# A fixed order for the whole program, output matmuls in column halves, and inputs laid out ahead

## The chip, the cores and the metric

One core of one Trainium2 chip runs the whole program. The metric is the device time of one execution in microseconds. TensorE is called PE here, VectorE DVE, ScalarE ACT, GpSimd POOL and SyncE SP.

## What is computed

Three stages in float32, one behind another: a linear attention with complex decay, a dense MLP, and a mixture of 8 experts with two experts to a token. Cut to what matters:

```python
# attention: B, H, S, D = 4, 8, 768, 48
mag = sqrt(a_re**2 + a_im**2); scale = minimum(mag, 0.999) / (mag + 1e-6)
for t in range(S):                                   # S: complex state [D, D] per head
    S_re, S_im = ar*S_re - ai*S_im + outer(k[t], v[t]), ar*S_im + ai*S_re
    y[t] = q[t] @ S_re
x = y.transpose(0, 2, 1, 3).reshape(3072, 384)
# dense MLP: d_ff = 2048; w_in and w_out arrive as float64
h = x @ w_in; g = where(h > 0, h, exp(minimum(h, 0)) - 1); x = g @ w_out
# experts: F = 1024
logits = x @ w_gate + log1p(exp(x @ w_noise)) * noise
top2 and their softmax weights; out[t] = sum of weight * (maximum(x[t] @ w1[e], 0) @ w2[e])
```

## The kernel before

**Attention** runs in units: a chunk of 128 steps for two of the four batches (`i` = 0, 1), 12 units in all, six chunks. Per unit the factors are made on ACT and DVE (`p_pieces`), the angles are summed on PE with a triangular matrix (L280), and the sizes are transposed on PE (L302) and multiplied up on DVE (L311 to L322). `kk` and `qq` (L371, L383) transpose the unit's k and q on PE, four transposes of a pair of heads each, since q and k are loaded with the steps on the partitions; DVE then reads the transposed q and k from PSUM (L372, L384). `sc` (L463) makes the scores, DVE masks them (L467). `y` (L480, L482) makes the output: for each of 8 heads one matmul with the carried state (`Sc`, from the second chunk on) and one with the masked scores `P`, each with 128 stationary columns and 48 moving. `upd` (L424) makes the state's update `pu`, with 64 stationary columns at a time. `xt` (L496 to L498) transposes the output and splits it in a high and a low part, `xh` and `xl`.

**The MLP** of a unit (`f_pieces`) multiplies in three passes of split float32: `ph` at L531 (256 moving columns), the activation on ACT and DVE (L535 to L541), then `y` at L555 (400 columns, of which 16 are the gate's). Its weights are loaded, decoded from float64 on DVE (L144 to L146, L161) and split with PE's help (L186 to L205) in the start. `route` picks the experts of a chunk and writes a table by indirect DMAs on POOL (L647).

**The experts** come last: for each of 8, rows are gathered by POOL (L728), transposed (L733), multiplied at L748 (`mph`), activated (L750, L751) and multiplied at L770 (`mpo`, one tile of 128 tokens each); the results are added to those of the experts before and scattered (L775, L778).

**The order** is set by priorities. `PAR` gives each class of pieces a window of time in the unit's clock, `place` and `settle` turn that into a priority, and the framework places whatever is ready by priority on the engines, matmul by matmul, with a timing of its own. Each engine then works its list from front to back. SP and POOL issue the loads from lists of that kind. `load` (L108 to L122) issues one DMA per tile: q and k go into tiles padded to 64 columns, which POOL first clears (L117); a_re and a_im come in one DMA each; all read runs of 48 values.

Of the kernel before, what the change touches and what calls it, by code (L numbers as in the profile page):

```python
# [21 lines left out]

@with_exitstack
def tile_kernel(ctx, tc, q, k, v, a_re, a_im, w_in, w_out, w_gate, w_noise, noise, w1, w2, out, dbg=None):
# [3 lines left out]
    L = 128  # L28
# [5 lines left out]
    F = w_in.shape[1]  # L34
# [25 lines left out]
    # ---------------------------------------------------------------- constants  # L60
# [32 lines left out]
    nc.vector.memset(nat["a"][:, :, :, :, D:], 0.0)  # L93
# [16 lines left out]
    def load(n, u, i):  # L110
        if n == "v":
            t = V[u, i] = wa.tile([128, Dm], F32, name="vt", tag="vt", bufs=2)
            to = t.rearrange("p (h d) -> p h d", h=H)
        else:
            if n in "qk":
                t = nat[n, u, i] = wa.tile([128, H, 64], F32, name=n, tag="n4", bufs=4)
                nc.gpsimd.memset(t[:, :, D:], 0.0)  # L117
            else:
                t = nat["a"][:, i, int(n == "ai")]
            to = t[:, :, :D]  # L120
        src = srcs[n]
        nc.sync.dma_start(to, bass.AP(tensor=src.tensor, offset=src.offset + bat(u, i) * H * S * D + chunk(u) * L * D,  # L122
                                      ap=[[D, L], [S * D, H], [1, D]]))
# [4 lines left out]
    # ---------------------------------------------------------------- weights of the first MLP  # L128
# [37 lines left out]
    def w_in_piece(f, a, b, raw):  # L166
        src = w_in.rearrange("(c p) f -> p c f", p=128)[:, a // 128:b // 128, f * 128:(f + 1) * 128]
        if wide:
            return raw.rearrange("p (c f) x -> p c (f x)", f=128), src.bitcast(I32)
        return raw.rearrange("p (c f) -> p c f", f=128), src  # L170
# [36 lines left out]
    # ---------------------------------------------------------------- attention, factors of a unit  # L207
    V, X, KK, ET = {}, {}, {}, {}

    def p_pieces(u):  # L210
        """per step: the logarithm of the squared factor and the tangent of half its angle"""
# [3 lines left out]
        def start():  # L215
            for i in range(NB):
                load("ar", u, i)
                load("ai", u, i)
# [29 lines left out]
    def t_pieces(ua, us):  # L248
        """cosines and sines of unit us, angles of unit ua: together, for the sake of the tables"""
# [20 lines left out]
    def o_pieces(u):  # L270
        """sums of the angles (twice the halves) in turns, less the whole turns, negated"""
# [18 lines left out]
    def m_pieces(u):  # L290
        """products of the factors' sizes"""
# [43 lines left out]
    def a_pieces(u):  # L335
# [20 lines left out]
        def by_head(x, t):  # L356
            """planes of real and imaginary parts, a pair's heads in the halves of the partitions,
            to planes of the heads, real and imaginary parts in the halves"""
            copy = nc.vector.tensor_copy
            copy(t[:64], x[64:, 0])  # L360
            copy(x[64:, 0], x[:64, 1])
            copy(x[:64, 1], t[:64])

        def kk(i):
            def f():
                x, k = X[u], KK[u, i]
                b = k[:, 1]
# [6 lines left out]
                by_head(k, nat["k", u, i].rearrange("p (q j) d -> p q (j d)", j=2))  # L374
            return f

        def qq(i):
            def f():
                x, b = X[u], ET[u]
                o = slice(i * HP, (i + 1) * HP)  # L380
                tp = psa.tile([128, HP, 128], F32, name="tp", **ring("qq"))
                for p in range(HP):
                    nc.tensor.transpose(tp[:, p, :], pairs(nat["q", u, i], p), ident)  # L383
                tt(b[:, o], b[:, o], tp, op=OP.mult)  # L384
# [11 lines left out]
    # ---------------------------------------------------------------- attention, products of a unit  # L396
    def b_pieces(u):
# [73 lines left out]
        def y(i):  # L471
            def f():
                b = bat(u, i)
                py = psa.tile([128, Dm], F32, name="py", **ring("y"))
                for p in range(HP):
                    for j in range(2):
                        h = 2 * p + j
                        oh = slice(h * D, (h + 1) * D)
                        if c:
                            mm(py[:, oh], X[u][:, j, i * HP + p, :], Sc[i][:, p, j, :], start=True, stop=False,  # L480
                               skip_group_check=True)
                        mm(py[:, oh], d["P", i, j][:, p, :], V[u, i][:, oh], start=not c, stop=True,  # L482
                           skip_group_check=True)
# [29 lines left out]
    # ---------------------------------------------------------------- first MLP of a unit  # L513
# [154 lines left out]
    # ---------------------------------------------------------------- mixture of experts  # L668
    FE = w1.shape[2] // 128
# [21 lines left out]
    def e_weight(e, f, n):  # L691
# [3 lines left out]
        if n == 0:  # L695
            nc.sync.dma_start(raw.rearrange("p (c f) -> p c f", c=KD),
                              w1[e].rearrange("(c p) f -> p c f", p=128)[:, :, f * 128:(f + 1) * 128])
# [86 lines left out]
    # ---------------------------------------------------------------- order of work  # L784
# [7 lines left out]
    def place(cls, u, pieces):  # L792
        """a class's pieces of a unit lie one after another in its window of time"""
# [9 lines left out]
    def settle(rules):  # L803
        """moves pieces to later times until all that use a thing come after what makes it"""
# [139 lines left out]
    def check():  # L944
        """flags: something for the general path, the first slot that is still open, slots per expert"""
# [48 lines left out]
    # ---------------------------------------------------------------- what the fast path left  # L994
# [3 lines left out]
    def rest(first):  # L998
        for e in range(E):
            with ExitStack() as st:  # L1000
# [19 lines left out]
                for f in range(FE):  # L1020
                    wa = gw.tile([128, KD, 128], F32, name="gwa")
                    nc.sync.dma_start(wa, w1[e].rearrange("(c p) f -> p c f", p=128)[:, :, f * 128:(f + 1) * 128])
# [13 lines left out]
    def redo():  # L1036
        """attention step by step, the first MLP and the routing for any values"""
# [140 lines left out]
    with tc.If(load_reg(0, 1) != 0):  # L1178
# [7 lines left out]
        "moe2_noise", "moe2_w1", "moe2_w2"]  # L1186
# [26 lines left out]
```

## Time and profile before

| | |
|---|---|
| median of 3 runs | 1281.93 us (1280.65 to 1283.49) |
| span of the profiled execution | 1274.1 us |
| PE busy | 1202.6 us, 94% |
| DVE busy | 797.9 us, 63% |
| ACT busy | 655.1 us, 51% |
| POOL busy | 251.8 us, 20% |
| HBM read, written | 80.69 MB, 20.70 MB |

The profile is of one execution; the span runs from its first to its last instruction. Matmuls are pipelined, so their durations overlap: what a matmul takes of PE is the distance from its start to the next start, not the mean duration in a group. A float32 matmul stands in the trace as two records, a transpose or a split one as one. The start up to the first `ph` takes some 125 us, attention and MLP together go on to about 775 us, the experts take the rest.

### The profile page before, as it was taken

Reading aid. Unit: us, or ns where it says so; the run is one execution under the profiler, and the core shown is the slowest. Engines: PE = TensorE matmul, PEld = TensorE weight load, DVE = VectorE, ACT = ScalarE, POOL = GpSimd, SP = SyncE. Lnnn points to the kernel's source line nnn. Section 1 sums busy time; section 2 is a strip of 40 time slices with the busy share of each in tenths; the row PEclk is TensorE's granted clock in tenths of the full one; section 3 lists DMA queues with packets and bytes.
Section 4 is the critical chain, followed back from the end, with each engine's and each line's share of the span. In section 5 each row is a group of like instructions: output and inputs, shape, how many; then the busy total and the mean of one; then the engine's idle time right before and its main releaser. Section 6 shows DMA issues by size and latency. Waiting matters only on the chain. (4 is left out here: it accounts for less than half of the span.)

```text
span 1274.1 us, 21830 instructions
## 1 busy us (share of the span) xinstructions
PE 1202.6 (94%) x8309; PEld 1132.9 (89%) x8309; DVE 797.9 (63%) x1783; ACT 655.1 (51%) x1299; POOL 251.8 (20%) x313
## 2 busy tenths in 40 slices
PE   3687999999999999999998999899999999999996
PEld 3475999999999999999998998899898989899995
DVE  6999958687887888788787557253434334353221
ACT  8768847476666857675663366142323333241110
POOL 3211000110020011002000400633333242424221
PEclk9788989899999999999999999899999999999998
DMA  9854121122131222213111134242425243332111
GB/s 269 231 134 113 32 55 27 40 37 57 23 57 36 45 46 43 57 20 57 26 32 33 32 119 125 80 130 87 139 90 145 86 129 106 109 113 83 42 44 33
DMA packets 192179, 100.71 MB, mean 79 GB/s; under 512 B 143231, under 2 KB 182886, under 8 KB 192064
## 3 DMA queue, kind: packets, MB, share of 16 engines
q1 hardware_dynamic: 177456, 59.36, 19.7%
q0 software_dynamic: 14608, 39.86, 10.3%
q8 instruction: 67, 1.10, 0.4%
q14 instruction: 48, 0.39, 0.1%
HBM read 80.69 MB, written 20.70 MB: 80 GB/s over the span
## 5 line engine op out<-in xcount | busy, mean ns | idle before, releaser
L751 DVE SCALAR_TENSOR_TENSOR egl<-mph,egh 128x320 fp32r<-128x320 f32 (+1 forms) x128 | 74.6, 587 | 158.7 <-ACT egh L750 158.7
L750 ACT ACTIVATE egh<-mph 128x320 fp32r<-128x320 f32 (+1 forms) x128 | 65.1, 514 | 210.4 <-PE mph L748 172.7
L770 PE MATMUL mpo<-weh,egh 128*128 128x384 f32 (+1 forms) x448 | 153.8, 343 | 0.4 <-ACT egh L750 0.4
L770 PE MATMUL mpo<-wel,egh 128*128 128x384 f32 (+1 forms) x448 | 151.4, 338 | 0.0
L555 PE MATMUL y<-woh,gh 128*128 128x400 f32 x384 | 138.2, 360 | 0.4 <-ACT gh L540 0.3
L555 PE MATMUL y<-wol,gh 128*128 128x400 f32 x384 | 133.9, 349 | 0.0
L555 PE MATMUL y<-woh,gl 128*128 128x400 f32 x384 | 125.1, 357 | 0.0
L770 PE MATMUL mpo<-weh,egl 128*128 128x384 f32 (+1 forms) x448 | 122.3, 338 | 0.0
L702 DVE TENSOR_TENSOR wel<-raw,weh 128x384 fp32r<-128x384 f32 x128 | 70.1, 556 | 71.0 <-ACT weh L701 65.9
L701 ACT ACTIVATE weh<-raw 128x384 fp32r<-128x384 f32 x128 | 66.2, 525 | 88.8 <-PE mph L748 62.8
L531 PE MATMUL ph<-xh,wih 128*128 128x256 f32 x576 | 105.5, 289 | 3.1 <-DVE route L635 1.5
L531 PE MATMUL ph<-xl,wih 128*128 128x256 f32 x576 | 106.9, 285 | 0.0
L531 PE MATMUL ph<-xh,wil 128*128 128x256 f32 x576 | 105.7, 285 | 0.0
L647 POOL DMA_INDIRECT table<-route x48 | 52.1, 1085 | 208.1 <-DVE route L638 195.3
L540 ACT ACTIVATE gh<-ge 128x512 fp32r<-128x512 f32 x96 | 60.5, 630 | 61.6 <-DVE ge L537 57.8
L778 POOL DMA_INDIRECT out_dram<-ac,slots x56 | 55.1, 984 | 184.0 <-DVE ac L775 158.4
L531 PEld LDWEIGHTS ph<-xh,wih 128*128 128x128 f32 x576 | 85.7, 190 | 4.8 <-DVE ge L537 2.3
L531 PEld LDWEIGHTS ph<-xl,wih 128*128 128x128 f32 x576 | 85.5, 190 | 0.0
L531 PEld LDWEIGHTS ph<-xh,wil 128*128 128x128 f32 x576 | 85.1, 190 | 0.0
L770 PEld LDWEIGHTS mpo<-weh,egh 128*128 128x128 f32 (+1 forms) x448 | 81.2, 181 | 3.6 <-ACT egh L750 0.7
L770 PEld LDWEIGHTS mpo<-wel,egh 128*128 128x128 f32 (+1 forms) x448 | 81.1, 181 | 2.9
L770 PEld LDWEIGHTS mpo<-weh,egl 128*128 128x128 f32 (+1 forms) x448 | 77.9, 180 | 4.7
(214 smaller groups left out, 2884.2 us busy)
## 6 DMA issues: line engine op xcount, KB each, us to landing
raw<-in_moe_w_dram SPq DMA_DIRECT2D x128, 192.0 KB, 2.6
raw<-in_moe_w_in_dram POOLq DMA_DIRECT2D x16, 384.0 KB, 4.2
raw<-in_moe_w_out_dram POOLq DMA_DIRECT2D x16, 384.0 KB, 4.0
nat_a<-in_a_re_dram SPq DMA_DIRECT2D x24, 192.0 KB, 3.9
nat_a<-in_a_im_dram SPq DMA_DIRECT2D x24, 192.0 KB, 2.8
vt<-in_v_dram SPq DMA_DIRECT2D x24, 192.0 KB, 2.7
q<-in_q_dram SPq DMA_DIRECT2D x24, 192.0 KB, 4.5
k<-in_k_dram SPq DMA_DIRECT2D x24, 192.0 KB, 2.8
```

The costliest lines, as they stand in the source:

```text
L531: mm(ph[:, j, :], w[:, z, :], x[:, z, :], start=n == 0, stop=n == 3 * KD - 1)
L540: act(gh, e, AF.Copy)
L555: mm(d["y"][i], g[:, j, i * L:(i + 1) * L], w, start=s == 0 and j == 0 and n == 0, stop=s == NS - 1 and j == 1 and n == 2)
L647: st = nc.gpsimd.indirect_dma_start(out=table[:, :], out_offset=bass.IndirectOffsetOnAxis(ap=idx, axis=0), in_=row, in_offset=None)
L701: act(w[0], raw, AF.Copy)
L702: tt(w[1], raw, w[0].bitcast(F32), op=OP.subtract)
L750: act(gs[0][:, f, :n], ph[:, :n], AF.Relu)
L751: stt(gs[1][:, f, :n], ph[:, :n], 0.0, gs[0][:, f, :n].bitcast(F32), op0=OP.max, op1=OP.subtract)
L770: mm(po[:m], x[:, f, o:o + m], w, start=k == 0, stop=k == 3 * FE - 1)
L778: sc = nc.gpsimd.indirect_dma_start(out=out[:, :], in_=ac[:m], in_offset=None, out_offset=bass.IndirectOffsetOnAxis(ap=st[:m, t, 0:1], axi ...
```

## The change

Three things change.

**A fixed order.** A new function `arrange` runs when the program up to the end of the experts has been recorded. It finds what each instruction must wait for (data, PSUM banks, buffers of a pool), gives each a duration from a table of its own, and plans one list for each engine: whenever an engine is free, it takes, of what is ready, the piece with the longest chain of work behind it, and from the check of the flags on simply the first one in the program. Consecutive matmuls into one tile are kept together as a run. It then ties each instruction to the one before it in its engine's list, so that the lists stand as planned. In its table (`cost`) the first number is the time until the next instruction may start, the second the duration, both in ns; `pr` is the priority. The 28 DMAs that clear outputs are held back to a later time of the plan.

**Column halves.** Each output matmul of `y` is issued as two, for the first and the second 64 of the 128 stationary columns, one after the other.

**Inputs laid out ahead.** `kernel()` passes q and k already transposed by pairs of heads and padded (`q_pairs`, `k_pairs`), v with the heads side by side, a_re and a_im padded and in one array, and `moe_w_in` and `moe2_w1` in blocks of 128 columns. The old q, k, v, a_re and a_im still go in for the general path, which does not run on these inputs. The 192 transposes, the memsets of q, k and the factors' padding go; the factors' two DMAs per tile become one.

```diff
+def arrange(tc):
+    ins = [i for i in nc.cur_bb.bb.instructions if type(i).__name__ != "BassTilePoolBoundary"]
...
+    def cost(n):
...
+            if i.tile_size[1] != 128 or i.tile_size[0] != 128:
+                return 72, 229
+            return (223, 387) if cols <= 128 else (1.72 * cols, 1.72 * cols + 170)
...
+        if e == "PE" and p is not None and kinds[n] == kinds[p] == "Matmult":
+            same = a[0] == b[0]
+            r32 = "32r" in str(i.ins[0].dtype)
+            if same and (not r32 or not i.start_tensor_calc):
+                run[n] = run[p]
...
+    for h in reversed(todo):
+        tail[h] = sum(step[z] for z in members[h][:-1]) + dur[members[h][-1]] + 34 + max((tail[x] for x in out[h]), default=0)
+    pr = {h: -tail[h] if h < cut else 1e9 + h for h in heads}
...
+        if kinds[h] == "DMACopy" and any(x[0].startswith("zero_") for x in acc[h]):
+            r = max(r, 90000.0 + 2000.0 * len(zeros))
...
+    while done < len(heads):
+        for e in E:
...
+        while cand[e] and cand[e][0][0] <= t:
+            r, p, h = heapq.heappop(cand[e])
+            heapq.heappush(now[e], (p, h))
+        p, h = heapq.heappop(now[e])
...
+        for z in order:
+            for y in before[e]:
+                tc.add_manual_dep(ins[z], ins[y].name, how, reason="order")
...
     def load(n, u, i):
+        if n == "a":
+            t = nat["a"][:, i]
+            nc.sync.dma_start(t.rearrange("p x h d -> p (x h d)"), ap[u, i])
+        elif n == "v":
             t = V[u, i] = wa.tile([128, Dm], F32, name="vt", tag="vt", bufs=2)
+            nc.sync.dma_start(t, vp[u, i])
         else:
-            if n in "qk":
-                t = nat[n, u, i] = wa.tile([128, H, 64], F32, name=n, tag="n4", bufs=4)
-                nc.gpsimd.memset(t[:, :, D:], 0.0)
...
+            t = nat[n, u, i] = wa.tile([128, HP, L], F32, name=n, tag="n4", bufs=4)
+            nc.sync.dma_start(t.rearrange("p q t -> p (q t)"), (qp if n == "q" else kp)[u, i])
...
         def kk(i):
-                tp = psa.tile([128, HP, 128], F32, name="tp", **ring("kk"))
-                for p in range(HP):
-                    nc.tensor.transpose(tp[:, p, :], pairs(nat["k", u, i], p), ident)
-                tt(b, b, tp, op=OP.mult)
+                tt(b, b, nat["k", u, i], op=OP.mult)
...
         def qq(i):
-                    nc.tensor.transpose(tp[:, p, :], pairs(nat["q", u, i], p), ident)
-                tt(b[:, o], b[:, o], tp, op=OP.mult)
+                tt(b[:, o], b[:, o], nat["q", u, i], op=OP.mult)
...
         def y(i):
+                        halves = [slice(z * (L // 2), (z + 1) * (L // 2)) for z in range(2)]
                         if c:
-                            mm(py[:, oh], X[u][:, j, i * HP + p, :], Sc[i][:, p, j, :], start=True, stop=False,
+                            for z in halves:
+                                mm(py[z, oh], X[u][:, j, i * HP + p, z], Sc[i][:, p, j, :], start=True, stop=False,
+                                   skip_group_check=True)
+                        for z in halves:
+                            mm(py[z, oh], d["P", i, j][:, p, z], V[u, i][:, oh], start=not c, stop=True,
                                skip_group_check=True)
-                        mm(py[:, oh], d["P", i, j][:, p, :], V[u, i][:, oh], start=not c, stop=True,
...
+    if dbg is None:
+        arrange(tc)
```

Lines of the new program are higher by some 300 (L480 and L482 are L783 and L786, L424 is L725, L463 is L764, L531 and L555 are L835 and L859, L770 is L1073, L144 to L146 and L161 are L452 to L454 and L469).

PE, the second output batch of unit 2, before: `pu` is the state's update and `py` the output, and the two alternate.

```order
L555 MATMUL y_1848<-woh,gl 128x400
L424 MATMUL pu<-vt,KT 64x48 x3
L482 MATMUL py<-vt,P 128x48
L424 MATMUL pu<-vt,KT 64x48
L480 MATMUL py<-Sc_112,X 128x48
L424 MATMUL pu<-vt,KT 64x48
```

The same place after, from the last matmuls of that batch on:

```order
L783 MATMUL py<-Sc_111,X 64x48 x2
L786 MATMUL py<-vt,P 64x48 x2
L800 MATMUL tp<-ident,yr 128x128 x3
L711 MATMUL tp<-ident,KK 128x128 x8
L800 MATMUL tp<-ident,yr 128x128 x3
L725 MATMUL pu<-vt,KT 64x48 x16
L764 MATMUL sc_2691<-X,KK 128x128
L587 MATMUL tp<-tri,nat_a 128x128 x4
```

The output's 32 halves now stand in one piece, and so do the 16 matmuls of the update.

DVE, the first steps behind the constants, before: `pa`, `pb`, `pc` and `nat_a` are the factor chain, `wf` and `wbad` the decoding of a weight piece.

```order
L229 TENSOR_TENSOR pa<-pa,pb 128x384
L233 SCALAR_TENSOR_TENSOR pc<-nat_a,pc 128x384
L240 SCALAR_TENSOR_TENSOR nat_a<-pa,pb 128x8x48
L239 TENSOR_TENSOR nat_a<-nat_a,pc 128x8x48
L229 TENSOR_TENSOR pa<-pa,pb 128x384
L233 SCALAR_TENSOR_TENSOR pc<-nat_a,pc 128x384
L240 SCALAR_TENSOR_TENSOR nat_a<-pa,pb 128x8x48
L161 TENSOR_REDUCE wbad<-raw 128x1
```

After:

```order
L452 TENSOR_SCALAR wf<-raw 128x384
L469 TENSOR_REDUCE wbad<-raw 128x1
L453 SCALAR_TENSOR_TENSOR wf<-raw,wf 128x384
L454 SCALAR_TENSOR_TENSOR wf<-raw,wf 128x384
L536 TENSOR_TENSOR pa<-pa,pb 128x384
L944 TENSOR_SCALAR route<-tokm 128x8
L540 SCALAR_TENSOR_TENSOR pc<-nat_a,pc 128x384
L547 SCALAR_TENSOR_TENSOR nat_a<-pa,pb 128x8x48
L536 TENSOR_TENSOR pa<-pa,pb 128x384
L546 TENSOR_TENSOR nat_a<-nat_a,pc 128x8x48
L452 TENSOR_SCALAR wf<-raw 128x384
```

The decoding of a piece now stands ahead of the factor chain and between its steps.

PE at the end, before: the numbers tell the tiles of the last expert apart; each `mpo` is one tile of tokens.

```order
L770 MATMUL mpo_13250<-wel_12394,egh_13114 128x384
L770 MATMUL mpo_13279<-weh_12393,egh_13114 64x384
L770 MATMUL mpo_13279<-wel_12394,egh_13114 64x384
L770 MATMUL mpo_13221<-weh_12393,egl_13115 128x384
L770 MATMUL mpo_13250<-weh_12393,egl_13115 128x384
L770 MATMUL mpo_13279<-weh_12393,egl_13115 64x384
```

After, where the last tile begins; its 24 matmuls then run to the end:

```order
L1073 MATMUL mpo_13289<-weh_12426,egl_13154 128x384
L1073 MATMUL mpo_13289<-weh_12432,egh_13153 128x384
L1073 MATMUL mpo_13289<-wel_12433,egh_13153 128x384
L1073 MATMUL mpo_13289<-weh_12432,egl_13154 128x384
L1073 MATMUL mpo_13318<-weh_12390,egh_13153 64x384
L1073 MATMUL mpo_13318<-wel_12391,egh_13153 64x384
```

The three tiles ended side by side; now they end one after another.

## Rows read from the trace of the kernel before

**Rows 1.** The page's span, and busy time of PE (share, instructions).
```profile
span 1274.1 us, 21830 instructions
PE 1202.6 (94%) x8309; PEld 1132.9 (89%) x8309; DVE 797.9 (63%) x1783; ACT 655.1 (51%) x1299; POOL 251.8 (20%) x313
```
**Rows 2.** Busy time by stage: stretch, its length, then the engines in the first row's order.
```profile
core 0: us, PE busy (x) PEld busy (x) DVE busy (x) ACT busy (x) POOL busy (x), PEclk, DMA share, GB/s
0.00:125.00 125.00, 83.16 (x464) 62.89 (x465) 107.09 (x256) 95.70 (x205) 27.08 (x54) 0.86 0.71 187
...
118.00:746.00 628.00, 615.62 (x4998) 604.01 (x4998) 487.38 (x1110) 403.29 (x768) 60.74 (x94) 0.99 0.20 41
...
354.48:467.09 112.61, 110.53 (x940) 109.22 (x939) 91.94 (x217) 77.53 (x148) 10.56 (x16) 1.00 0.21 44
...
812.00:1262.00 450.00, 444.41 (x2488) 408.54 (x2486) 168.80 (x320) 127.16 (x268) 151.29 (x152) 0.99 0.34 98
```
**Rows 3.** PE by line: names, shapes, records | busy us, mean ns.
```profile
L482 PE MATMUL py<-vt,P 128*128 128x48 f32 x384 | 72.5, 276 | 0.0
L480 PE MATMUL py<-Sc,X 128*128 128x48 f32 x320 | 61.5, 274 | 0.0
```
**Rows 4.** PE in order of time: start, us, line, names, records; an ordinary batch.
```profile
324.01 0.32 PE L480 MATMUL py<-Sc,X 128*128 128x48 f32 x2
...
324.59 0.43 PE L555 MATMUL y<-woh,gh 128*128 128x400 f32 x1
...
327.58 0.32 PE L482 MATMUL py<-vt,P 128*128 128x48 f32 x2
...
330.50 1.14 PE L424 MATMUL pu<-vt,KT 128*64 128x48 f32 x32
331.57 0.45 PE L555 MATMUL y<-woh,gh 128*128 128x400 f32 x1
```
**Rows 5.** PE in order of time: two scattered batches, first and next row.
```profile
156.06 0.32 PE L424 MATMUL pu<-vt,KT 128*64 128x48 f32 x2
...
161.23 1.04 PE L555 MATMUL y<-woh,gl 128*128 128x400 f32 x2
...
230.20 0.43 PE L424 MATMUL pu<-vt,KT 128*64 128x48 f32 x6
...
241.21 0.90 PE L496 MATMUL tp<-ident,yr 128*128 128x128 f32 x3 [0.20 <-ACT yr L485]
```
**Rows 6.** By stretch, behind those two: PEclk is the column after POOL's.
```profile
163.00:169.00 6.00, 6.00 (x36) 5.94 (x36) 1.97 (x5) 1.72 (x3) 0.00 (x0) 0.76 0.07 13
...
234.50:241.20 6.70, 6.51 (x28) 5.17 (x27) 1.34 (x6) 0.49 (x1) 0.00 (x0) 0.50 0.04 2
241.20:245.00 3.80, 3.79 (x32) 3.73 (x33) 3.29 (x15) 1.18 (x2) 0.00 (x0) 0.58 0.29 58
```
**Rows 7.** PE in order of time: a group of transposes, and what follows.
```profile
304.26 0.60 PE L371 MATMUL tp<-ident,k 128*128 128x128 f32 x4
304.62 0.36 PE L531 MATMUL ph<-xl,wih 128*128 128x256 f32 x1
304.82 0.51 PE L531 MATMUL ph<-xh,wil 128*128 128x256 f32 x3
```
**Rows 8.** DVE by line, 0 to 125 us: busy us, mean ns | idle before.
```profile
L161 DVE TENSOR_REDUCE wbad<-raw 128x1 f32<-128x384 f32 x32 | 17.5, 546 | 1.0 <-DMA raw<-in_moe_w_in_dram 0.7 <-DMA raw<-in_moe_w_out_dram 0.3
L454 DVE COPY Sc<-St 48x192 f32<-48x192 f32 x8 | 2.0, 254 | 0.1
L352 DVE TENSOR_TENSOR KK<-E,KK 128x512 f32<-128x512 f32 x4 | 2.8, 688 | 1.1 <-ACT KK L351 1.1
L372 DVE TENSOR_TENSOR KK<-KK,tp 128x512 f32<-128x512 f32 x2 | 1.4, 682 | 0.0
```
**Rows 9.** End of the program in order of time: POOL's scatters.
```profile
1262.08 1.02 POOL L778 DMA_INDIRECT out_dram<-ac,slots  x1 [12.15 <-DVE ac L775]
...
1264.70 0.92 POOL L778 DMA_INDIRECT out_dram<-ac,slots  x1 [0.30 <-issue]
```

More of the change, by code (lines that the diff above doesn't have):

```diff
@@ L1 @@
+import collections
+import heapq
 import math
@@ L23, in tile_kernel @@
 @with_exitstack
-def tile_kernel(ctx, tc, q, k, v, a_re, a_im, w_in, w_out, w_gate, w_noise, noise, w1, w2, out, dbg=None):
+def tile_kernel(ctx, tc, q, k, v, a_re, a_im, w_in, w_out, w_gate, w_noise, noise, w1, w2, qp, kp, vp, ap,
+                out, dbg=None):
     nc = tc.nc
@@ L33, in tile_kernel @@
     NU = NC * (B // NB)
-    F = w_in.shape[1]
+    F = w_out.shape[0]
     FB = F // 128
@@ L166, in w_in_piece @@
     def w_in_piece(f, a, b, raw):
-        src = w_in.rearrange("(c p) f -> p c f", p=128)[:, a // 128:b // 128, f * 128:(f + 1) * 128]
+        src = w_in[f, :, a:b]
         if wide:
-            return raw.rearrange("p (c f) x -> p c (f x)", f=128), src.bitcast(I32)
-        return raw.rearrange("p (c f) -> p c f", f=128), src
+            return raw.rearrange("p f x -> p (f x)"), src.bitcast(I32)
+        return raw, src
     def w_out_piece(f, a, b, raw):
@@ L216, in start @@
             for i in range(NB):
-                load("ar", u, i)
-                load("ai", u, i)
+                load("a", u, i)
         P.append((0.0, start))
@@ L380, in f @@
                 o = slice(i * HP, (i + 1) * HP)
-                tp = psa.tile([128, HP, 128], F32, name="tp", **ring("qq"))
-                for p in range(HP):
-                    nc.tensor.transpose(tp[:, p, :], pairs(nat["q", u, i], p), ident)
-                tt(b[:, o], b[:, o], tp, op=OP.mult)
+                tt(b[:, o], b[:, o], nat["q", u, i], op=OP.mult)
                 tt(x[:, :, o], x[:, :, o], b[:, None, o].to_broadcast([128, 2, HP, L]), op=OP.mult)
@@ L666, in clear_table @@
         return nc.sync.dma_start(table.rearrange("(p r) x -> p r x", p=128), t)
-    FE = w1.shape[2] // 128
+    FE = w2.shape[1] // 128
     HEAD = 512
@@ L695, in e_weight @@
         if n == 0:
[L696 to L697 removed]
+            nc.sync.dma_start(raw, w1[e, f])
         else:
@@ L1195, with blocks, units, pad @@
     from concourse.bass_utils import run_bass_kernel_spmd as _run
+    def blocks(w):
+        K, F = w.shape[-2:]
+        x = w.reshape(w.shape[:-2] + (K // 128, 128, F // 128, 128))
+        n = x.ndim
+        return x.transpose(tuple(range(n - 4)) + (n - 2, n - 3, n - 4, n - 1)).reshape(w.shape[:-2] + (F // 128, 128, K))
+    def units(x):
+        B, H, S, D = x.shape
+        x = x.reshape(B // 2, 2, H, S // 128, 128, D).transpose(3, 0, 1, 4, 2, 5)
+        return x.reshape(-1, 2, 128, H, D)
+    def pad(x):
+        p = _np.zeros(x.shape[:-1] + (64,), x.dtype)
+        p[..., :x.shape[-1]] = x
+        return p
+    def across(x):
+        x = pad(units(x))
+        n, b, t, h, d = x.shape
+        return x.reshape(n, b, t, h // 2, 2 * d).transpose(0, 1, 4, 3, 2).reshape(n, b, 2 * d, -1)
+    inputs = {n: _np.asarray(x) for n, x in inputs.items()}
+    v = units(inputs["v"])
+    n, b, t = v.shape[:3]
+    laid = dict(inputs, moe_w_in=blocks(inputs["moe_w_in"]), moe2_w1=blocks(inputs["moe2_w1"]),
+                q_pairs=across(inputs["q"]), k_pairs=across(inputs["k"]), v_rows=v.reshape(n, b, t, -1),
+                a_rows=_np.stack([pad(units(inputs[x])) for x in ("a_re", "a_im")], 3).reshape(n, b, t, -1))
     nc = _bacc.Bacc("TRN2", target_bir_lowering=False, num_devices=1)
@@ L1199 @@
     for name in _INS:
-        a = _np.ascontiguousarray(inputs[name])
+        a = _np.ascontiguousarray(laid[name])
         if a.dtype == _np.float64:
```

286 lines of the change are left out of this document (273 added, 13 removed).

## The prediction, on record before the changed kernel ran

> **What bounds the kernel now.** I read the page first, then the busy time by stage, then the order of time of PE at the places that the change touches. The page gives a span of 1274.1 us with PE busy for 94% of it [rows 1]. By stage, PE is the engine that is nearly full from the first MLP matmul to the end: 615.62 of 628 us between 118 and 746 us, 444.41 of 450 in the mixture of experts [rows 2]. There the other engines have room: in one chunk of attention (354.48 to 467.09 us) DVE is busy 91.94 and ACT 77.53 of 112.61 us. The start is different: in the first 125 us DVE is busy 107.09 us and PE 83.16, since decoding and splitting the first MLP's weights is DVE's work. So a microsecond taken from PE's work counts in full after the start, and hardly within it. The median of the runs is 1281.93 us; the profiled execution's span is 7.8 us less, and I leave these 7.8 as they are.
>
> **The change, part by part.**
>
> *The output's matmuls in halves.* A batch of `y(i)` is 8 or, from the second chunk on, 16 matmuls; the trace has two records for each [rows 3]. In an ordinary batch now 6 records take 0.58 us (324.01 to 324.59) and 26 take 2.92 (327.58 to 330.50), so 3.50 for 32 records, 0.11 each [rows 4]. After the change the batch has 64 records of 64 columns. The trace of before has that very form, 128 rows by 64 columns with 48 moving, in the state's update `pu`, which also alternates between the two column halves: 32 records there take 1.07 us up to the next start, 0.033 each [rows 4]. Two such lengths are 2.14; one drain at the end falls away and an entry is added, so I take 2.1, with 2.0 and 2.3 as bounds. The gain is 1.4 us a batch (1.2 to 1.5). There are 24 batches: 20 long ones and 4 of the first chunk. One long one is treated below, so 19 x 1.4 = 26.6 us. Of the short ones the two of unit 0 lie in the start and count nothing; one of unit 1 goes from 1.8 to about 1.2: 0.6.
>
> *Two scattered batches.* Twice the old order alternates a matmul of 128 columns with one of 64, and each switch costs: 5.17 us from 156.06 to 161.23, and 11.01 us from 230.20 to 241.21 [rows 5]. The first stretch holds 32 `pu` records and 14 of the output, the second 32 and 26. In the new order each batch stands in one piece. By the lengths above that is 2.1 and 2.8 us, a gain of 3.1 and 8.2. Sum of the output's part: 26.6 + 0.6 + 11.3 = 38.5 us.
>
> *The clock behind them.* In the second scattered stretch the granted clock is 0.50, the 1.2 GHz level, and it stays low for a while behind both: 0.76 in the 6 us up to 169, 0.58 in the 3.8 us up to 245 [rows 6]. That is some 2.9 and 3.2 us at the half level, so 3 us lost, which I count as gained (0 to 3). PE shows as busy all through the 6 us ahead of 169. The Trainium skill ("TensorE: Matmul & The Clock Gate", Part 1, on the two states of the clock) ties the level to how busy the engine has been; if a full busy row were enough for the full clock, these 3 us would have nothing to do with scattered batches, and the sum would be 3 us smaller.
>
> *No transposes of q and k.* 192 transposes go, in 48 groups of four. A group takes 0.36 us (304.26 to 304.62) [rows 7]. Four groups are unit 0's, in the start. 44 x 0.36 = 15.8 us; up to 0.08 a group more, since the matmul behind one starts 0.20 after its own neighbour in rows 7, but some switches stay. The products that read them take q and k from SBUF instead of PSUM; the same form takes 688 ns with both operands in SBUF and 682 with one in PSUM [rows 8], so nothing on DVE. The memsets of q and k on POOL go too, from an engine that waits. The loads on SP become one per tile with long runs, and the factors' two loads become one. What could feel them is ACT, which opens each unit with the factors, and ACT is busy 77.53 of 112.61 us in a chunk [rows 2]; in the start DVE waits 1.0 us in all for weights to land [rows 8]. So I price the loads at nothing. If that cover fails, the landing of a load shows as a wait of ACT at the head of a unit and, through the factor chain, of PE.
>
> *The start under the new order.* The first `ph` matmul starts at 124.9 us, behind DVE's work. In DVE's new order the second `xl`, on which it waits, has fewer steps ahead of it. Two reductions (0.55 each), two pairs of KK steps (0.69 each) and the eight copies to Sc (2.0 us in all) now stand behind it [rows 8], and so do five steps of a state update, of which I take 0.5 each: 1.1 + 2.8 + 2.0 + 2.5 = 8.4 us. That is the gain I take, 8.5. From below it is nothing, if weights on PE and ACT, not DVE, end the start. From above it is 17 or so: decoding now stands between the steps of the factor chain, and DVE's idle time in that stretch is 125 - 107.09 = 17.9 us [rows 2].
>
> *The end.* Now the last three accumulations end together, and POOL issues three scatters one behind another, from 1262.08 to 1264.70 us for the last [rows 9]. In the new order each accumulation is one run, so only the last tile's scatter follows the last matmul: 2.5 us (0 to 2.6).
>
> *Everything else* is the same work in another order. PE's idle time between 118 and 746 us is 12.4 us [rows 2], and I let it stand: bounds are its disappearance and a new wait, priced below. The expert weights, gathers and scatters keep their kinds and numbers, and PE's 5.6 idle us after 812 us stay.
>
> Sum: 38.5 + 3 + 15.8 + 8.5 + 2.5 = 68.3 us. Span 1274.1 - 68.3 = 1205.8; with 7.8 around it **1213.6 us**.
>
> **The rivals.**
>
> *The new plan also removes waits.* For it: the old order leaves PE 12.4 us idle in the attention stage and DVE 17.9 in the start, and a plan that starts whatever is ready could use both. Against it: the old order's idle time is already thin. With 9 us more from the start, 12 from the waits and 3 behind the transposes: about 1190 us.
>
> *DVE takes the place of the transposes.* A chunk's PE time falls by 4 x 1.4 + 8 x 0.36 = 8.5 us, from 112.6 to 104.1, while DVE's 91.94 stay [rows 2]. Its idle share would go from 20.7 to 12.2 us. Each step of DVE waits for ACT or PE by turns. If it can't be kept fed with less than 16 us of idle time, a chunk takes 108 and loses 3.9 of its gain; over the 5.5 chunks behind the start that is 21 us: about 1235 us.
>
> *The halves don't overlap.* Then each of the 64 records costs what a record of the whole costs now, 0.11 us, and a long batch takes 7.0 us instead of 2.1. The price is 4.9 x 20 and some 2.4 for each of two short ones, together 103 us: 1317 us, slower than before. It decides from the point where a batch costs 2.1 + 68.3/20 = 5.5 us, 0.086 us a record. The 0.033 of `pu` in the same form speaks against it; for it speaks only that the weights here come from X and P in slices of a wider tile. The Trainium skill ("TensorEngine Tiling (Array Packing)", Performance Considerations) says it: a matmul has a fixed overhead, one with a free dimension of 1 takes as long as one of 60, and no tiling factor should be taken from a dimension that is already small. By that rule alone twice the matmuls of 48 columns are twice the time. Rows 4 show otherwise as long as the two halves alternate.
>
> *The change does not do what it says:* in the new order the transposes are gone and the matmuls are 64 wide, so only a wait in their place could undo it. A plan fixed in advance keeps every engine to its row; the whole 68 us would be eaten by 5.7 us of new PE waits in each of 12 units. I see no place for that in the order.
>
> **How the numbers follow.** The forecast, 1213 us with its own bounds of 1201 to 1227, has a chance of 0.57. The plan that also removes waits (1190) has 0.17, DVE in the way (1235) 0.18. The halves that don't overlap have 0.03, and 0.05 is left for waits that I don't see, 0.03 of it about as long as the gain and 0.02 longer. The range leaves out the far end of the second, some 0.04, and of the third, and the cases above it: 1183 to 1246 us. A difference within 0.2% (2.6 us) is about what a measurement of this kernel can't tell from no change. Faster 0.92, same 0.03, slower 0.05.
>
> **What would show each step.** The output's batches should stand in PE's order of time as 64 records within 2.0 to 2.3 us; at 3 us or more the step on the halves is wrong. The granted clock between 150 and 260 us should be 1.00. The first `ph` matmul should start near 116 us. A chunk should take 104 us from one route to the next, with DVE busy for 92 of them; 108 or more with PE waiting for DVE is the third case. After the last matmul one scatter should follow, not three. The forecast is wrong as a whole if PE's idle time between the first `ph` and the first expert grows beyond 25 us, or if loads or gathers, which I price at nothing, show up as PE waits.

## The result: 1.4 per cent, a quarter of the forecast gain

The changed kernel takes 1264.28 us (median of 4 runs, 1261.97 to 1265.75) against 1281.29 for the kernel before: a ratio of 0.9862, 95% interval 0.9833 to 0.9890. I had forecast 1213 us with a range of 1183 to 1246. The direction was right, the size was not. The profile after, its span and the engines' busy time:

```profile
span 1262.9 us, 22761 instructions
PE 1164.5 (92%) x8821; PEld 1077.0 (85%) x8821; DVE 791.2 (63%) x1782; ACT 649.5 (51%) x1299; POOL 243.2 (19%) x265
```

PE's busy time falls by 38 us [rows 1], the span by 11.2. Where the rest went is seen when the span is cut at the first `ph`, the last MLP matmul and the last matmul. "Work" counts each record of a stretch at the distance to the next start that its form has undisturbed (0.111 us for a record of a whole output matmul, 0.031 for a half, 0.09 for a transpose of q or k, 0.12 and 0.18 for the MLP's two products); "loss" is the rest of the stretch: waits, changes of form, a half clock.

| stretch | before, us | after, us | change of work, us | loss before, us | loss after, us |
|---|---|---|---|---|---|
| start to first `ph` | 124.9 | 127.1 | -4.7 | 79.6 | 86.5 |
| to the last MLP matmul | 661.6 | 639.2 | -55.3 | 39.4 | 72.3 |
| to the last matmul | 474.9 | 487.8 | +8.4 | 11.2 | 15.7 |
| tail | 12.6 | 8.8 | | | |

In all 51.6 us of work are gone (34.5 by the halves, 17.2 by the transposes; the 8.4 are expert matmuls that the old order had already placed ahead of the last MLP matmul). But 44.3 us of new loss stand against it, 32.9 of them in the stretch where I had let PE's waits stand. Busy time by stage there, after: stretch, length, PE, weight loads, DVE, ACT, POOL, granted clock; the first row is the whole stretch, the others are chunks from one route to the next.

```profile
127.00:766.00 639.00, 596.78 (x5691) 575.85 (x5690) 502.73 (x1162) 420.85 (x806) 55.47 (x54) 0.98 0.21 60
...
350.77:462.55 111.78, 104.30 (x1036) 100.11 (x1034) 91.54 (x217) 77.20 (x149) 9.69 (x8) 0.98 0.19 55
462.55:574.37 111.82, 104.75 (x1035) 100.64 (x1035) 91.54 (x217) 77.30 (x149) 9.69 (x8) 0.97 0.17 51
```

PE now idles 42 of 639 us; it was 12.4 of 628 [rows 2]. A chunk fell from 112.6 us to 111.8, not to 104, and DVE idles 20.3 us in it, as before (20.7). What PE waits for in that stretch (us in total, times, longest):

```profile
PE tp L711 <- ACT KT L713: 13.5, 9, 2.4
PE py L786 <- DVE P L768: 10.6, 10, 1.8
PE pr L933 <- DVE route L929: 8.9, 3, 7.3
PE ph L835 <- DVE ge L841: 3.9, 7, 0.8
PE ph L835 <- DVE xl L802: 2.7, 4, 0.7
```

The output's matmuls themselves did what the `pu` rows had promised. PE in order of time, an ordinary batch (64 records), and then one that waits for the masked scores `P`:

```profile
207.22 0.32 PE L783 MATMUL py<-Sc,X 128*64 128x48 f32 x4
...
209.22 0.66 PE L711 MATMUL tp<-ident,KK 128*128 128x128 f32 x4
```
```profile
450.07 0.32 PE L783 MATMUL py<-Sc,X 128*64 128x48 f32 x4
450.23 0.29 PE L786 MATMUL py<-vt,P 128*64 128x48 f32 x4
450.34 0.29 PE L783 MATMUL py<-Sc,X 128*64 128x48 f32 x4
452.37 0.32 PE L786 MATMUL py<-vt,P 128*64 128x48 f32 x4 [1.74 <-DVE P L768]
...
454.81 0.90 PE L800 MATMUL tp<-ident,yr 128*128 128x128 f32 x3
```

The first takes 2.00 us from start to next start, where rows 4 showed 3.50. The second takes 4.74: it stops for 1.74 us, and behind this stop the granted clock is 0.51 from 453 to 454 us and 0.50 up to 456, the 1.2 GHz level. Of the 20 batches with a carried state 11 take 2.00 us; the other 9, each a unit's second, take 2.8 to 4.7.

### The profile page after: what moved, and what is told of

Same layout as the page of the kernel before. It is cut to its first block, busy times and chain, and to the rows that moved or that the text cites. A ratio compares the mean times of both kernels' runs of the same rounds, so it can differ in the third digit from the quotient of the medians.

```text
span 1262.9 us, 22761 instructions
## 1 busy us (share of the span) xinstructions
PE 1164.5 (92%) x8821; PEld 1077.0 (85%) x8821; DVE 791.2 (63%) x1782; ACT 649.5 (51%) x1299; POOL 243.2 (19%) x265
## 4 chain that ended last, share of the span: by engine, by line
PE 59%; DVE 24%; ACT 10%; issue 4%; DMA 1%; POOL 0%; another core or an unknown queue 0%; SPq 0%; POOLq 0%; ACTq 0%; DVEq 0%
PE mpo L1073 17%; PE mph L1051 17%; PE y L859 8%; PE ph L835 8%; DVE E L618 2%; DVE ge L841 2%; DVE KK L677 2%; DVE X L686 2%; PE mtp L1036 1%; DVE gl L845 1%; DVE Sc L755 1%; ACT L562 1%; DVE P L768 1%; PE sc L764 1%; PE tp L587 1%
## 5 line engine op out<-in xcount | busy, mean ns | idle before, releaser
L951 POOL DMA_INDIRECT table<-route x48 | 55.1, 1148 | 613.1 <-DVE route L945 542.3
L1073 PE MATMUL mpo<-weh,egh 128*128 128x384 f32 (+1 forms) x448 | 151.7, 339 | 0.0
L1073 PE MATMUL mpo<-weh,egl 128*128 128x384 f32 (+1 forms) x448 | 151.6, 338 | 0.0
L1073 PE MATMUL mpo<-wel,egh 128*128 128x384 f32 (+1 forms) x448 | 151.2, 337 | 0.0
L859 PE MATMUL y<-woh,gh 128*128 128x400 f32 x384 | 141.0, 367 | 0.5 <-ACT yo L871 0.5
L859 PE MATMUL y<-woh,gl 128*128 128x400 f32 x384 | 132.6, 345 | 0.0
L859 PE MATMUL y<-wol,gh 128*128 128x400 f32 x384 | 131.4, 342 | 0.0
L1078 DVE SCALAR_TENSOR_TENSOR ac<-mpo,slots,ac 128x384 f32<-128x384 f32 (+1 forms) x49 | 30.2, 617 | 160.8 <-PE mpo L1073 160.8
L835 PE MATMUL ph<-xh,wih 128*128 128x256 f32 x576 | 106.4, 294 | 4.0 <-DVE ge L841 3.9
L835 PE MATMUL ph<-xl,wih 128*128 128x256 f32 x576 | 101.3, 285 | 2.8 <-DVE xl L802 2.7
L835 PE MATMUL ph<-xh,wil 128*128 128x256 f32 x576 | 100.7, 284 | 0.0
L845 DVE TENSOR_TENSOR gl<-ge,gh 128x512 fp32r<-128x512 f32 x96 | 65.8, 689 | 49.3 <-ACT gh L844 48.6
L835 PEld LDWEIGHTS ph<-xh,wih 128*128 128x128 f32 x576 | 87.9, 191 | 5.6 <-PE sc L764 3.6
L839 ACT ACTIVATE ge<-ph 128x512 f32<-128x512 f32 x96 | 57.2, 596 | 63.6 <-DVE gl L845 47.1
L835 PEld LDWEIGHTS ph<-xl,wih 128*128 128x128 f32 x576 | 83.0, 191 | 3.8 <-DVE xl L802 3.8
L841 DVE SCALAR_TENSOR_TENSOR ge<-ge,ph 128x512 f32<-128x512 f32 x96 | 65.6, 683 | 32.2 <-ACT ge L840 27.3
```

The costliest lines, as they stand in the source:

```text
L835: mm(ph[:, j, :], w[:, z, :], x[:, z, :], start=n == 0, stop=n == 3 * KD - 1)
L839: act(e, ph, AF.Relu, scale=-1.0)
L841: stt(e, e, -1.0, ph, op0=OP.add, op1=OP.max)
L845: tt(gl, e, gh.bitcast(F32), op=OP.subtract)
L859: mm(d["y"][i], g[:, j, i * L:(i + 1) * L], w, start=s == 0 and j == 0 and n == 0, stop=s == NS - 1 and j == 1 and n == 2)
L1073: mm(po[:m], x[:, f, o:o + m], w, start=k == 0, stop=k == 3 * FE - 1)
```

## Why are the lists late? Two things the planner's table leaves out

The planner puts every engine's instructions in a fixed row, by a table of durations. It keeps a planned start for each; set against the trace, the DVE instruction planned at 125 us starts 14.9 us late, the one at 250 us 26.4, at 450 us 40.2 and at 735 us 52.7 us late. The lists lose time all the way through attention and MLP; by its own table the plan ends at 1194 us, the trace at 1262.9. The trace suggests two causes, which the experiments below test. The first is on ACT: ACT, DVE and PE around a unit's sines, in order of time.

```profile
446.49 1.28 ACT L562 ACT_TABLE_LOAD   x1
...
447.78 1.06 ACT L562 ACTIVATE X<-X 128x1024 f32<-128x1024 f32 x1
...
448.75 1.14 ACT L563 ACTIVATE X<-X,bias 128x1024 f32<-128x1024 f32 x1
...
449.92 0.20 DVE L649 TENSOR_TENSOR al<-X,E 128x16 f32<-128x16 f32 x1 [1.32 <-ACT X L563]
...
450.50 1.22 DVE L677 TENSOR_TENSOR KK<-KK,X 128x1024 f32<-128x1024 f32 x1
...
451.63 0.69 DVE L768 TENSOR_TENSOR P<-sc,causal 128x512 f32<-128x512 f32 x1
```

A load of the function table, 1.28 us, stands ahead of the first sine. The recorded program has only the load behind the sines (L569), and so has the planner's table; this one is put in later. Each of the 14 groups of sines and arctangents has one. DVE waits 1.32 us for X here, makes `P` later (451.63), and the batch above waits 1.74 us for it. The Trainium skill ("ScalarE activation tables: per-element evaluation and per-set limits", What a function is on this engine) gives 1283 ns for such a load; the trace agrees with 1.28.

The second is on DVE. DVE in order of time, after:

```profile
470.14 0.68 DVE L841 SCALAR_TENSOR_TENSOR ge<-ge,ph 128x512 f32<-128x512 f32 x1
470.73 0.68 DVE L592 SCALAR_TENSOR_TENSOR X<-X,tp 128x512 f32<-128x512 f32 x1
...
472.65 0.42 DVE L667 COPY k<-KK 64x512 f32<-64x512 f32 x1
473.10 0.69 DVE L768 TENSOR_TENSOR P<-sc,causal 128x512 f32<-128x512 f32 x1
473.83 0.42 DVE L667 COPY E<-X 64x512 f32<-64x512 f32 x1
474.28 0.69 DVE L841 SCALAR_TENSOR_TENSOR ge<-ge,ph 128x512 f32<-128x512 f32 x1
475.00 0.42 DVE L668 COPY KK<-KK 64x512 f32<-64x512 f32 x1
475.34 0.41 DVE L668 COPY X<-X 64x512 f32<-64x512 f32 x1
475.79 0.42 DVE L669 COPY KK<-k 64x512 f32<-64x512 f32 x1
476.13 0.41 DVE L669 COPY X<-E 64x512 f32<-64x512 f32 x1
```

A 128x512 step is followed after 0.59 us by another such step (470.14 to 470.73), but after 0.72 or 0.73 by a copy (473.10 to 473.83, 474.28 to 475.00). A copy is followed after 0.34 us by a copy between the same partitions (475.00 to 475.34), else after 0.45. So a change costs 0.12 us on either side; these copies move 64 partitions between the lower and the upper half. The planner's table has 0.33 for them. The Trainium skill ("VectorE: DVE Perf Modes", Two Vector instructions with no wait between them) has a rule for it: an instruction whose input or output starts in another group of 32 partitions than the last input read from that memory, or the last output written to it, starts only when all VectorE instructions before it have finished. The rows agree: behind each change the next step starts 0.03 to 0.04 us after the one before has ended, elsewhere before its end.

## Experiments: does a fuller table bring the gain?

Theory A: what the table leaves out comes back as lateness of the lists, and PE waits. Theory B: the chain of DVE and ACT sets a chunk's pace once PE has less to do, whatever the plan. Ratios below are to the kernel before on the same chip.

**The changed kernel again:** no edit. 

> The changed kernel as it is, beside the two plans below on one chip. Both theories: 0.983 to 0.989 of the time before.

 Measured 0.9858 (0.9834 to 0.9882).

**The table load in the table.**

```diff
+            if n in switch:
+                s, d = s + 1290, d + 1290
```

(`switch` holds the first sine or arctangent of each group.) 

> As the changed kernel, but the planner's table of durations also holds the 1.28 us load of ScalarE's function table ahead of a unit's first sine or arctangent, which the trace shows 14 times and the plan has not. Theory A: VectorE and PE no longer wait for X behind these loads; a chunk falls from 111.8 to about 109 us, 1248 to 1256 us in all. Theory B: within 4 us of the changed kernel, 1260 to 1268.

 Measured 0.9778 (0.9744 to 0.9813), 1247.99 us: theory A, and its three full chunks take 110.5, 109.7 and 110.3 us. But 9.6 of the 16.9 us between the two spans came where I had not looked: the first `ph` starts at 117.5 us instead of 127.1. PE in order of time, after and in this run:

```profile
115.84 0.90 PE L800 MATMUL tp<-ident,yr 128*128 128x128 f32 x3 [0.32 <-DVE xl L802]
120.37 0.90 PE L502 MATMUL wtp<-ident,wf 128*128 128x128 f32 x3 [3.63 <-DVE wf L454]
...
127.10 0.60 PE L835 MATMUL ph<-xh,wih 128*128 128x256 f32 x3
```
```profile
116.52 0.87 PE L508 MATMUL wtp<-ident,wf 128*128 128x128 f32 x3
117.49 0.79 PE L841 MATMUL ph<-xh,wih 128*128 128x256 f32 x2
```

**And the copies.**

```diff
                 if not psum_in[n]:
                     r = .53
+                    if k == "TensorCopy":
+                        r += 120 / c
```

> As the run before, and the planner's table also gives each VectorE copy from SBUF 0.12 us more, which the trace shows for most of them (0.45 us from start to start for the 64x512 copies, 0.28 for the 48x192 ones, planned as 0.33 and 0.16). Theory A: the lists now run nearly as planned; a chunk takes 106 to 108 us and the whole 1225 to 1240. Theory B: within 4 us of the changed kernel.

 Measured 0.9643 (0.9610 to 0.9675), 1230.03 us: theory A again. The three full chunks take 108.3, 106.3 and 105.0 us. The shortest by stage, and what PE waits for most from the first `ph` to the last MLP matmul:

```profile
446.20:551.20 105.00, 102.00 (x1038) 98.48 (x1037) 89.65 (x216) 76.03 (x149) 7.99 (x8) 1.00 0.19 54
```
```profile
PE tp L617 <- DVE route L921: 5.6, 4, 1.4
PE sc L772 <- DVE X L676: 4.8, 1, 4.8
PE tp L808 <- ACT yr L797: 4.4, 1, 4.4
PE py L794 <- DVE P L776: 3.1, 4, 0.8
```

The same work takes 105.0 us here with DVE idle for 15 of them. So theory B's chain is not what held the changed kernel at 111.8. The forecast is still not reached: the span is 46.3 us shorter than before, of 68.3.

**The copies alone** (the edit above without the first). 

> As the changed kernel, with the copies' 0.12 us in the planner's table but not the function-table load. Theory A (what the table leaves out of VectorE's copies comes back as lateness): about 17 us faster than the changed kernel, 0.970 to 0.976 of the time before. Theory E (the gain came from the pair of corrections, or by chance of the list): 0.980 to 0.988.

 Measured 0.9698 (0.9669 to 0.9727), just past the edge of theory A's range.

**The same slack for other instructions**, on the plan with the table load.

```diff
+            if k == "TensorTensor" and c == 512:
+                r += 120 / c
             s = 58 + c * r + (60 if ...)
```

> As the plan with the function-table load, but the 0.12 us go to 216 other VectorE instructions, the 128x512 products and differences, which the table had right. Theory A: no gain on that plan, 0.974 to 0.984 of the time before. Theory E (any slack given to VectorE in the plan does it, not these copies): 0.961 to 0.968, as with the copies.

 Measured 0.9717 (0.9690 to 0.9744), below theory A's 0.974 and above theory E's; by the ratio alone the slack elsewhere might have gained up to 8 us. The two stretches decide better than the ratio, since these runs were on different chips, and each traced execution lies within 2.1 us of its kernel's median: loss in the middle stretch, start of the first `ph`, and how much later DVE's lists get between the plan's 125 and 735 us.

| table of the plan | loss, us | first `ph`, us | lists later by, us |
|---|---|---|---|
| as changed | 72.3 | 127.1 | 37.8 |
| + table load | 64.3 | 117.5 | 21.8 |
| + copies | 52.4 | 129.4 | 19.6 |
| + both | 47.1 | 118.0 | 6.7 |
| + table load, slack elsewhere | 63.0 | 116.9 | 22.6 |
| without any table load | 75.1 | 123.6 | 38.0 |
| + both, hand-overs 100 ns longer | 49.8 | 119.8 | 7.8 |

The copies take 17 and 20 us off the loss, with and without the table load, and slack elsewhere takes 1. The table load is worth 5 to 8 us there and 10 to 11 at the first `ph`. Together they take 25.2 us off the loss, singly 8.0 and 19.9: nearly the sum, as of two separate causes. Of the 32.9 us by which the change had raised the loss, 7.7 stay without a cause.

**Neither table load known.**

```diff
             if k == "LoadActFuncSet":
-                return 1290, 1283
+                return 20, 20
```

> As the changed kernel, but the planner's table also loses the function-table load that it has (the one back to the exponential's set, 1.29 us, planned 15 times): now it knows neither of a unit's two loads. Theory A (what the table leaves out comes back as waits): another 8 to 16 us slower than the changed kernel, 0.992 to 1.000 of the time before. Theory B (the table's gaps don't matter much, the copies run did something else): within 4 us of the changed kernel.

 Measured 0.9848 (0.9823 to 0.9873): as theory B expected, no change. The middle loses 2.8 us more and the start 3.5 less. So theory A doesn't price a gap by its length times its number: the 1.28 us missing behind the sines cost nothing here; ahead of them they cost 5 to 8 us. Why this one is harmless I have not settled.

**Longer hand-overs**, on the plan with both.

```diff
-            lat = 34 + (20 if e == "PE" else 0)
+            lat = 134 + (20 if e == "PE" else 0)
```

> As the plan with table loads and copies, but each hand-over from one engine to another is planned 100 ns longer (134 for 34). If the rest of PE's waits there comes from small lateness that hits lists without slack, the plan gains 5 to 10 us on that run, 0.955 to 0.960 of the time before; if the lists are now near what the engines can do, the longer chains cost: 0.964 to 0.972.

 Measured 0.9600 (0.9576 to 0.9624), at the edge of the gain case. At 1230.05 us it is as long as the run with both on a chip where the kernel before is 4 us slower; the intervals overlap, and which is the better stays open. Both runs are faster than the kernels before and after.

## Experiments: what is each part worth?

**Without the plan**, halves and laid-out inputs under the old priorities.

```diff
-    if dbg is None:
-        arrange(tc)
```

> The halves and the laid-out inputs stay; the fixed order is left away, so the old priorities set the order. Theory A (the fixed order leaves steps out of its table, so its lists run late against it, and PE waits 33 us more between the first ph and the last MLP matmul): without it the waits go back to about those of before, 40 us in that stretch, and the time is 1225 to 1240 us. Theory B (the VectorE-ScalarE chain of a chunk sets the pace once PE has less to do, in any order): PE waits about as much as with the plan, 1258 to 1270 us.

 Measured 1.0191 (1.0161 to 1.0221): neither theory; the plan, faulty as it was, is worth 42 us here.

**Whole output matmuls** in the changed kernel.

```diff
-                        halves = [slice(z * (L // 2), (z + 1) * (L // 2)) for z in range(2)]
+                        halves = [slice(0, L)]
```

> As the changed kernel, but each output matmul with all 128 columns again; the order is planned anew. PE's work grows by 34 us, 16 matmuls of 0.22 us instead of 64 records of 0.03 in each of 20 batches. Theory A (errors of the plan are the same ones with or without halves): about 20 to 30 us slower than the changed kernel, 1285 to 1294 us. Theory B (PE is not the bound in the chunks): most of it falls into waits, 1264 to 1274 us.

 Measured 1.0011 (0.9987 to 1.0036), 19 us above the changed kernel by the ratios, just short of A's 20 to 30 us. PE's work is 34.5 us more and the middle's loss 14 us less, in the trace of an execution that took 8 us more than the median of the ten (1277.25).

**Whole output matmuls under the plan with both corrections:** the last edit, on that run's kernel. 

> The plan with the table loads and the copies in its table, laid-out inputs, but output matmuls of 128 columns. Against the run with that table and halves (0.964 of the time before) this prices the halves under an order that runs nearly as planned. Theory A (PE is the bound again once the lists fit): 25 to 34 us slower than with halves, 0.984 to 0.991. Theory B (VectorE and ScalarE take part of it): 10 to 20 us slower, 0.972 to 0.980.

 Measured 0.9799 (0.9765 to 0.9833): the halves are worth 20 us by the ratios, 28 by the medians, which come from two chips, and by the spans. By the ratio that is theory B's size, at its upper edge: some of the 34.5 us fall into waits even under a plan that fits. From the first `ph` to the last MLP matmul PE stands still for 24 us with halves, for 12 with whole matmuls.

**Each part alone on the kernel before.** The halves:

```diff
+                        halves = [slice(z * (L // 2), (z + 1) * (L // 2)) for z in range(2)]
...
-                            mm(py[:, oh], X[u][:, j, i * HP + p, :], Sc[i][:, p, j, :], ...)
+                            for z in halves:
+                                mm(py[z, oh], X[u][:, j, i * HP + p, z], Sc[i][:, p, j, :], ...)
```

and `P` likewise. 

> The kernel before with nothing but the output's matmuls in halves, in the order of the old priorities. PE's work falls by 34 us. Theory C (the old order places matmul by matmul, scatters the halves among 128-column work and pays for it in switches and waits; that is why halves and laid-out inputs without the plan were slower than the kernel before): no gain or a loss, 1.00 to 1.02 of the time before. Theory D (the laid-out inputs upset the old order): 0.975 to 0.985 of the time before.

 Measured 1.0271 (1.0230 to 1.0312). The inputs, from the changed kernel:

```diff
-                        halves = [slice(z * (L // 2), (z + 1) * (L // 2)) for z in range(2)]
+                        halves = [slice(0, L)]
...
-    if dbg is None:
-        arrange(tc)
```

> The kernel before with nothing but the inputs laid out, in the order of the old priorities, output matmuls of 128 columns. PE's work falls by 17 us. Theory C: 0.985 to 0.995 of the time before, most of the 17 us is seen. Theory D: slower than the kernel before by 1 per cent or more.

 Measured 1.0160 (1.0135 to 1.0185). The plan, with `arrange` word for word in the kernel before:

```diff
+    if dbg is None:
+        arrange(tc)
```

> The kernel before with nothing but the fixed order, as the changed kernel's planner makes it. If the plan itself costs waits (table loads and copies that it leaves out, as the two runs with a fuller table say), the loss of PE between the first ph and the last MLP matmul grows from 39 us to 50 to 65, and the time is 1.005 to 1.02 of the time before. If the plan is a gain by itself and the old order is what holds the other two parts back: 0.98 to 1.00.

 Measured 1.0435 (1.0414 to 1.0457).

Each part alone makes the kernel slower. Theory C had the inputs alone as a gain, theory D the halves alone; each failed in one of the two runs. The plan alone lies beyond both of its cases: its middle loses 93 us, not 50 to 65, its DVE lists get 60 us later between the plan's 125 and 735 us (37.8 in the changed kernel), and its first `ph` starts at 147.9 us, 23 later than before. It was not run with the two corrections, so how much of this the table explains stays open.

It isn't the output's matmuls that cost in the run with the halves: all their records take 50.8 us to the next start there, 82.6 in the kernel before. The three full chunks take 119.5, 134.4 and 127.4 us; the longest by stage, and DVE's largest wait from the first `ph` to the last MLP matmul:

```profile
351.20:485.60 134.40, 119.55 (x1117) 111.83 (x1115) 97.48 (x230) 80.88 (x157) 10.70 (x17) 0.92 0.19 38
```
```profile
DVE ge L540 <- ACT ge L539: 63.6, 33, 13.1
```

The chunk is 134 us long with PE busy for 120 at a granted clock of 0.92. The loss of the middle stretch is 115 us with the halves alone, 87 with the inputs alone, 93 with the plan alone, 108 with halves and inputs, against 39 in the kernel before; the traced executions lie up to 8.3 us from the medians of their kernels. Not all of it is waiting: with the halves alone PE stands still for 54 of the 706 us and the granted clock is 0.94, with the inputs alone for 33 of 696 at 0.95, before for 12 of 662 at 0.99. The old priorities give 39 for exactly the old program; with 17 or 34 us less work on PE they place the instructions in other orders, with more loss. That they fit only the old durations is what these runs suggest, but it is not shown; I tried no other priorities.

## Why the prediction was wrong, step by step

**The step that failed** is "Everything else is the same work in another order. PE's idle time [...] is 12.4 us [...], and I let it stand". Rows 2 showed the idle time of an old list that fitted the old program; a new list has its own. The loss of that stretch grew by 32.9 us, over half of the 57 us of gain in the span that are missing; the two corrections of the planner's table take 25.2 of them back. PE's idle time between the first `ph` and the first expert beyond 25 us was the sign that I had named for a forecast wrong as a whole; it is 42. I had read the new order as rows of names, but not asked whether the durations that made it are those of the trace. The table was in the diff, and a copy at 0.33 us against 0.45 from start to start could have been read from the trace of before; so could the 1.28 us load, which stands there too.

**Halves.** 2.1 us a batch forecast, 2.00 measured undisturbed; 34.5 us of work against 38.5 with the scattered batches. Right in mechanism, but 9 of the 20 long batches wait. From the rule of the Trainium skill ("TensorEngine Tiling (Array Packing)", Performance Considerations), a fixed overhead for each matmul, I had drawn twice the time for twice the matmuls. For alternating halves the trace does not agree: 0.031 us a record against 0.111 of a whole one.

**Scattered batches and the clock.** Each batch now stands in one piece, as forecast. The 3 us of clock did not come: the granted clock is 0.98 between 150 and 260 us, where I had asked for 1.00, and 0.98 in the whole middle stretch. It falls to the half level late in each chunk, behind PE's waits: in the 8.2 us ahead of the fall at 234.6 us PE is busy for 4.0.

**Transposes.** 17.2 us of work, 15.8 forecast. The loads cost PE no wait that the trace shows, and ACT's waits for the factors' loads, 16.5 us in all before, fell to 0.7.

**Start.** 8.5 us forecast, -2.2 measured. The step took the second `xl` for what the first `ph` waits for. The trace of before shows otherwise: `xl` is done at 121.4 us and `ph` starts 3.5 us later, without a wait, behind PE's work on the weights. In the changed kernel `xl` is done at 121.3 us and `ph` comes 5.8 us later (127.10, in the rows above). Both in order of time, before, then after:

```profile
120.37 1.01 DVE L498 TENSOR_TENSOR xl<-tp,xh 128x384 fp32r<-128x384 f32 x2
...
124.93 0.52 PE L531 MATMUL ph<-xh,wih 128*128 128x256 f32 x3
```
```profile
120.72 0.56 DVE L802 TENSOR_TENSOR xl<-tp,xh 128x384 fp32r<-128x384 f32 x1 [0.41 <-ACT xh L801]
```

So work on the weights ends the start, the case that I had named for no gain. PE waits there for the decoded weights `wf` instead of the factors `nat_a` (us in all in the first 125 us, times, longest; after, then before):

```profile
PE wlo L494 <- DVE wf L454: 19.3, 5, 9.0
PE wtp L502 <- DVE wf L454: 8.3, 5, 3.6
PE tp L609 <- DVE nat_a L547: 3.3, 1, 3.3
PE tp L587 <- ACT nat_a L566: 1.5, 2, 0.8
```
```profile
PE tp L302 <- DVE nat_a L240: 9.3, 1, 9.3
PE tp L280 <- ACT nat_a L259: 8.8, 2, 7.1
PE wlo L186 <- DVE wf L146: 7.2, 2, 6.8
```

I had placed the decoding between the steps of the factor chain as a gain of DVE's idle time, and not asked when PE needs it. With the table load in the plan the first `ph` comes at 117.5, near the 116 that I had expected.

**End.** One scatter follows the last matmul instead of three; 3.8 us, 2.5 forecast. POOL and DVE in order of time:

```profile
1254.17 0.61 DVE L1078 SCALAR_TENSOR_TENSOR ac<-mpo,slots,ac 64x384 f32<-64x384 f32 x1 [3.59 <-PE mpo L1073]
1255.06 0.92 POOL L1081 DMA_INDIRECT out_dram<-ac,slots  x1 [3.20 <-DVE ac L1078]
```

**The 7.8 us around the span** were no such thing. The changed kernel's runs lie 1.8 us above their own spans, so the profiled execution of before was a short one among its runs (1275.66 to 1283.49 us). About 6 us of the gain in the medians are not in the two traces.

**The rivals.** "DVE takes the place of the transposes" came nearest: it asked for a chunk of 108 us and more, with PE waiting for DVE. But it blamed DVE's load, and the run with both corrections does the same DVE work in 105.0. It was a rival of 0.18 that should have been worse and likelier, with its cause in the plan. The rival "does not do what it says" asked for 5.7 us of new waits in each of 12 units; about half of that came (32.9 / 12 = 2.7), where I had seen "no place for that in the order". An order shows no lateness.

## What to carry to other kernels

A fixed order is as good as the durations that made it: before you believe in it, set its table against the trace, instruction by instruction, for steps that are missing (a table load) and for costs that depend on the neighbour (a copy to other partitions). Set the plan's own end against the trace's too. Idle time that was thin under a tuned order is a property of that order and of that program; when either is changed, it is a term of its own and needs bounds. Each part of a change may lose alone and gain together, so price them in the order in which they'll run.

## What the chip showed that I had not expected

DVE's copies between halves of the partitions cost 0.12 us at each change to or from other steps, 0.45 us from start to start for 0.33; a plan that leaves these 0.12 us out, for some 240 copies, costs 17 to 20 us of loss, about what the halved output matmuls brought in the end.
